# Two MLPs behind a retention layer: token blocks of 512 and 384, and the first weight conversions in another place

## The chip, the cores and the metric

One core of one Trainium2 chip. The time is the device time of one launch in microseconds (us). Three runs of the kernel before took 967.38, 970.62 and 971.07 us; the median is 970.62 us.

## The reference

```
scores = q @ k.T / sqrt(D);  ret = scores * Dmat        # Dmat = gamma_h ** (i - j) for i >= j, else 0
x  = heads side by side of ret @ v                      # 4 batches x 576 rows = 2304 tokens of 512
h  = x @ w_in;  x = (h * sigmoid(1.702 * h)) @ w_out                 # 512 -> 2048 -> 512
xn = x / sqrt(mean(x * x) + 1e-6) * rms_g
out = (silu(xn @ w_gate) * (xn @ w_val)) @ w_out2                    # 512 -> 1536 -> 512
```

All tensors are float32, and the weights too.

## The kernel before

Each matmul is done three times on fp32r operands: every operand is split into a high part and a rest, and `three` (lines 190 to 195) adds high x high, high x rest and rest x high into one PSUM tile. So one projection of 512 inputs onto 128 outputs is twelve matmuls whose moving operand is as wide as the token block.

**Blocks.** The first MLP goes through the 2304 tokens in blocks of 512, 448, 448, 448 and 448 (`BLOCKS`), the second in six blocks of 384 (`NB`). For each of the 16 (second MLP: 12) groups f of 128 hidden units, `m1_up` makes twelve matmuls into `h`, ACT and DVE apply the gate (`g`) and split it (`gh`, `gl`), and `m1_down` makes twelve more into four accumulators `acc`. `m2_up` makes twelve into `h` and twelve into `v`, and `m2_down` nine of 512 columns (three tiles of 128 tokens, three matmuls each). Down runs two groups behind up (`LAG`). Before each up, `w_rot` splits the group's output weights on ACT (`wrh`, line 186) and DVE (`wrl`, line 187).

**Attention.** The retention is done in units of at most 128 rows that end where a batch or a token block ends: 20 units, four of them of 64 rows. A unit is three phases: `a_trans` (transposes on TensorE, copies `kT` and `qT` on ACT), `a_scores` (matmuls of kT and qT, mask on DVE into `r`) and `a_out` (matmuls, then `x`, the carried state `S` and the split into `xh` and `xl`). Block 0's four units are done first; those of block n+1 are laid between the groups of block n by the table `gap` (lines 654 to 657): for block 0 phase i of the list goes to group 2 + i*14 // len(list).

**Weights.** They arrive as 64-bit words and are converted by `conv`: two passes on ACT (lines 159, 160), one on DVE (line 169), and for `in`, `gate` and `val` a cast and a difference on DVE (lines 176, 177). They are staged in six slots `sslots` and kept in 56 slots of 2 KB per partition. While block 0 runs, `conv_next(2)` converts one `in` and one `out` piece ahead of each group; the first two pieces are converted between attention phases (lines 640 and 642).

**Order.** Everything is written out by hand (`manual_schedule`): each engine works its queue off in the order of the code, and waits at the head of the queue hold all that is behind.

Of the kernel before, what the change touches and what calls it, by code (L numbers as in the profile page):

```python
# [8 lines left out]

F32 = mybir.dt.float32  # L10
F32R = mybir.dt.float32r
BF16 = mybir.dt.bfloat16
I32 = mybir.dt.int32
U32 = mybir.dt.uint32
U8 = mybir.dt.uint8
# [1 line left out]
ALU = mybir.AluOpType  # L17
PSUM = bass.MemoryType.PSUM

BLOCKS = (512, 448, 448, 448, 448)  # L20
NB = 384
XB = max(BLOCKS)
LAG = 2
NSLOT = 56
NMORE = 4
NSTG = 6
MAGIC = 0x5F3759DF
# [25 lines left out]
def kernel(  # L53
# [23 lines left out]
    KD = DM // 128  # L77
    NF1 = DF1 // 128
    NF2 = DF2 // 128
    NBLK = NT // NB  # L80
    N1 = len(BLOCKS)
    assert sum(BLOCKS) == NT
    TPB = NB // 128
# [3 lines left out]
    xp = ctx.enter_context(tc.tile_pool(name="xp", bufs=1))  # L87
    gp = ctx.enter_context(tc.tile_pool(name="gp", bufs=2))
    dram = ctx.enter_context(tc.tile_pool(name="dram", bufs=1, space=bass.MemoryType.DRAM))
    ps_acc = ctx.enter_context(tc.tile_pool(name="ps_acc", bufs=4, space=PSUM))  # L90
# [34 lines left out]
    staged = {}  # L125

    def w_free(key, f):
        wfree.extend(i for i, _ in W.pop((key, f)))

    def w_load(key, f):  # L130

# [18 lines left out]
    def words(key, f):  # L150
# [2 lines left out]
        b = sslots[:, i, :].bitcast(U8).rearrange("p (c t) -> p c t", t=8)  # L153
        return t[:, :, 0].bitcast(U32), t[:, :, 1], b[:, :, 3]

    def conv(pieces):
        for p in pieces:
            lo, hi, byte = words(*p)
            nc.scalar.activation(out=hi, in_=hi, func=AF.Prelu, scale=2.0 ** -112, alpha=-(2.0 ** 32))
            nc.scalar.activation(out=lo, in_=byte, func=AF.Copy, scale=1 / 32, bias=-31 / 64)  # L160
        for key, f in pieces:
            lo, hi, _ = words(key, f)
            if key in by_rows:
                W[key, f] = [w_slot("w")]
                w = W[key, f][0][1]
            else:
                W[key, f] = [w_slot("w") for _ in range(2)]
                w = gp.tile([128, 512], F32, tag="ww", name="ww", bufs=1)
            nc.vector.scalar_tensor_tensor(  # L169
                out=w.bitcast(U32), in0=hi.bitcast(U32), scalar=3, in1=lo,  # L170
                op0=ALU.logical_shift_left, op1=ALU.bitwise_or,
            )
            sfree.append(staged.pop((key, f)))
            if key not in by_rows:
                (_, wh), (_, wl) = W[key, f]
                nc.vector.tensor_copy(out=wh.bitcast(F32R), in_=w)  # L176
                nc.vector.tensor_tensor(out=wl.bitcast(F32R), in0=w, in1=wh, op=ALU.subtract)
# [26 lines left out]
    def block_tile(n):  # L204
        if n not in xt:
            xt[n] = (
                xp.tile([128, KD, BLOCKS[n % 2]], F32R, tag=f"xh{n % 2}", name="xh"),
                xp.tile([128, KD, BLOCKS[n % 2]], F32R, tag=f"xl{n % 2}", name="xl"),
            )
        return xt[n]  # L210

    aslots = {}
    hfree = deque()
    keep = [0]

    def a_tile(u, name):

        if len(wfree) > keep[0]:
            aslots[u, name], t = w_slot(name)
            return t  # L220
        if not hfree:
            i = sfree.popleft()
            hfree.extend([(i, 0), (i, 1)])
        i, j = aslots[u, name] = hfree.popleft()
        return sslots[:, i, j * 512:(j + 1) * 512]

    def a_free(u, *names):
        for nm in names:
            slot = aslots.pop((u, nm))
            if isinstance(slot, tuple):  # L230
                hfree.append(slot)
                if sum(i == slot[0] for i, _ in hfree) == 2:
                    hfree.remove((slot[0], 0))
                    hfree.remove((slot[0], 1))
                    sfree.append(slot[0])
            else:
                wfree.append(slot)

    def a_load(u, what="kqv"):
        b, s, c = units[u]  # L240
# [174 lines left out]
            )  # L415


    def halves(ids, c=NB):

        return [sslots[:, i, :2 * c].rearrange("p (k c) -> p k c", k=2) for i in ids]  # L420

# [17 lines left out]
    xraw = {}  # L439
    ssq = {}  # L440

    def norm_tile(name):
        return sp.tile([128, NB], F32, tag="norm", name=name, bufs=3)

    def m2_load(n):
        xraw[n] = [sfree.popleft() for _ in range(2)]
        for i, t in enumerate(halves(xraw[n])):
            nc.sync.dma_start(out=t, in_=y_d[:, 2 * i:2 * i + 2, n * NB:(n + 1) * NB])

    def m2_squares(n, i):  # L450

        y = halves(xraw[n])[i]
        if i == 0:
            ssq[n] = norm_tile("ssq"), norm_tile("sq")
        a, b = ssq[n]
        for j in range(2):
            o = a if i == j == 0 else b
            nc.gpsimd.tensor_tensor(out=o, in0=y[:, j, :], in1=y[:, j, :], op=ALU.mult)
            if o is b:
                nc.gpsimd.tensor_tensor(out=a, in0=a, in1=b, op=ALU.add)  # L460

    def m2_norm(n):

        y = halves(xraw[n])
        ps = ps_h.tile([128, XB], F32, tag="h", name="h")[:, :NB]
        nc.tensor.matmul(ps, ones, ssq.pop(n)[0], start=True, stop=True)
        m, r, t = (norm_tile(nm) for nm in ("m", "r", "t"))
        nc.vector.tensor_scalar(out=m, in0=ps, scalar1=1e-6, scalar2=None, op0=ALU.add)

        def guess():  # L470
# [21 lines left out]
    def m2_back(n):  # L492

        ids = xraw.pop(n)
        for i, t in enumerate(halves(ids)):
            nc.sync.dma_start(out=y_d[:, 2 * i:2 * i + 2, n * NB:(n + 1) * NB], in_=t)
        sfree.extend(ids)

    def m2_split(n, i):
        if n not in x2:  # L500
            x2[n] = (
                xp.tile([128, KD, BLOCKS[(N1 + n) % 2]], F32R, tag=f"xh{(N1 + n) % 2}", name="xh"),
                xp.tile([128, KD, BLOCKS[(N1 + n) % 2]], F32R, tag=f"xl{(N1 + n) % 2}", name="xl"),
            )
        xh, xl = x2[n]
        t = halves(xraw[n])[i]
        sfree.append(xraw[n][i])
        ks = slice(2 * i, 2 * i + 2)
        nc.scalar.copy(out=xh[:, ks, :NB], in_=t)
        nc.vector.tensor_tensor(  # L510
            out=xl[:, ks, :NB], in0=t, in1=xh[:, ks, :NB].bitcast(F32), op=ALU.subtract
        )

    def m2_up(n, f, fill):
        pg = ps_h.tile([128, XB], F32, tag="h", name="h")[:, :NB]
        proj(pg, "gate", f, x2[n], NB)
        g = hidden(F32, "g", NB, 2)
        nc.scalar.activation(out=g, in_=pg, func=AF.Sigmoid)  # L518
        nc.vector.tensor_tensor(out=g, in0=pg, in1=g, op=ALU.mult)  # L519
        pv = ps_v.tile([128, NB], F32, tag="v", name="v")  # L520
        proj(pv, "val", f, x2[n], NB)
        nc.vector.tensor_tensor(out=g, in0=pv, in1=g, op=ALU.mult)  # L522
        split_hidden((2, n, f), g, NB, fill)

    def m2_down(n, f):
        if f == 0:
            acc[n] = [ps_acc.tile([128, 512], F32, tag="acc", name="acc") for _ in range(4)]
        w = R.pop(("out2", f))
# [30 lines left out]
    with tc.manual_schedule():  # L559
# [220 lines left out]
```

## Time and profile before

| | |
|---|---|
| profiled execution, device time | 968.6 us |
| its span | 966.8 us |
| median of the three runs | 970.62 us |
| TensorE matmul busy | 953.6 us, 99% |
| DVE, ACT, POOL busy | 543.1, 376.7, 98.5 us |

The span goes from the first to the last instruction. TensorE's busy time is a union of overlapping matmuls, so the rate at which matmuls are issued has to be read from stretches that hold a known number of them.

### The profile page before, as it was taken

How to read it: one execution, taken by the hardware profiler on the slowest of the kernel's cores; microseconds unless marked ns; L12 is line 12 of the kernel's file. 1: busy time of each engine (PE TensorE's matmuls, PEld its weight loads, DVE VectorE, ACT ScalarE, POOL GpSimd, SP SyncE). 2: the span in 40 equal slices, each digit the busy share in tenths (PEclk: the TensorE clock that was granted, in tenths of full speed). 3: DMA queues.
4: the chain of work that ended last, by engine and by line, in shares of the span. 5: the costliest groups of instructions: out<-in, count | busy, mean ns of one | idle time of the engine just before them, and what ended most of it. 6: DMA issues, size and time to landing. Idle time of an engine off the chain costs nothing.

```text
span 966.8 us, 14045 instructions
## 1 busy us (share of the span) xinstructions
PE 953.6 (99%) x5654; PEld 860.8 (89%) x5654; DVE 543.1 (56%) x890; ACT 376.7 (39%) x688; POOL 98.5 (10%) x105
## 2 busy tenths in 40 slices
PE   9899999999999999999999999999999999999998
PEld 8687888889888989899999889999999999999997
DVE  3777754444446444367787785754654564554433
ACT  3566653334333433346665433232223223223322
POOL 3101111010311000100000330300110020000000
PEclk9999999999999999999999999999999999999999
DMA  9876502120211223006465301002001000000000
GB/s 233 211 218 180 148 17 77 33 52 18 85 34 50 65 55 126 23 36 199 122 194 190 89 1 66 1 1 66 1 1 55 12 1 11 23 1 1 33 1 33
DMA packets 92240, 66.77 MB, mean 69 GB/s; under 512 B 58896, under 2 KB 85648, under 8 KB 92176
## 3 DMA queue, kind: packets, MB, share of 16 engines
q1 hardware_dynamic: 92176, 65.89, 24.5%
q8 instruction: 44, 0.72, 0.3%
q14 instruction: 20, 0.16, 0.1%
HBM read 55.65 MB, written 10.22 MB: 68 GB/s over the span
## 4 chain that ended last, share of the span: by engine, by line
PE 89%; DVE 7%; ACT 2%; issue 1%; DMA 1%; DVEq 0%; ACTq 0%
PE h L193 12%; PE acc L195 11%; PE acc L194 11%; PE h L195 11%; PE h L194 11%; PE acc L193 11%; PE v L194 5%; PE v L195 5%; PE v L193 5%; PE at L286 2%; PE at L327 2%; PE at L261 2%; PE at L317 1%; DVE ww L169 1%; DVE w L176 1%
## 5 line engine op out<-in xcount | busy, mean ns | idle before, releaser
L193 PE MATMUL h<-xh,w 128*128 128x384 f32 (+2 forms) x608 | 223.0, 367 | 1.5 <-ACT xh L363 1.5
L194 PE MATMUL h<-xl,w 128*128 128x384 f32 (+2 forms) x608 | 216.2, 356 | 2.0 <-DVE xl L510 1.7
L195 PE MATMUL h<-xh,w 128*128 128x384 f32 (+2 forms) x608 | 216.7, 356 | 0.0
L378 ACT CAST gh<-g 128x384 fp32r<-128x384 f32 (+2 forms) x152 | 83.2, 547 | 252.6 <-DVE g L522 167.7
L380 DVE TENSOR_TENSOR gl<-g,gh 128x384 fp32r<-128x384 f32 (+2 forms) x152 | 94.2, 620 | 81.4 <-ACT gh L378 81.4
L187 DVE TENSOR_TENSOR wrl<-w,wrh 128x512 fp32r<-128x512 f32 x152 | 107.0, 704 | 56.2 <-ACT wrh L186 56.0
L193 PEld LDWEIGHTS h<-xh,w 128*128 128x128 f32 x608 | 114.6, 188 | 14.2 <-ACT xh L363 1.6
L194 PEld LDWEIGHTS h<-xl,w 128*128 128x128 f32 x608 | 114.7, 189 | 12.6 <-DVE xl L510 2.4
L195 PEld LDWEIGHTS h<-xh,w 128*128 128x128 f32 x608 | 114.4, 188 | 7.3
L186 ACT CAST wrh<-w 128x512 fp32r<-128x512 f32 x152 | 94.0, 619 | 68.2 <-PE acc L195 48.2
L195 PE MATMUL acc<-gh,wrl 128*128 128x448 f32 (+1 forms) x320 | 119.0, 372 | 0.6 <-DVE wrl L187 0.6
L194 PE MATMUL acc<-gl,wrh 128*128 128x448 f32 (+1 forms) x320 | 118.9, 371 | 0.0
L193 PE MATMUL acc<-gh,wrh 128*128 128x448 f32 (+1 forms) x320 | 118.8, 371 | 0.0
L402 DVE TENSOR_TENSOR g<-h,g 128x448 f32<-128x448 f32 (+1 forms) x80 | 50.8, 635 | 107.6 <-ACT g L401 107.5
L193 PE MATMUL v<-xh,w 128*128 128x384 f32 x288 | 96.2, 334 | 0.0
L195 PE MATMUL v<-xh,w 128*128 128x384 f32 x288 | 96.2, 334 | 0.0
L194 PE MATMUL v<-xl,w 128*128 128x384 f32 x288 | 96.2, 334 | 0.0
L401 ACT ACTIVATE g<-h 128x448 f32<-128x448 f32 (+1 forms) x80 | 44.3, 554 | 116.3 <-PE h L195 116.2
L194 PE MATMUL acc<-wrl,gh 128*128 128x512 f32 x216 | 85.4, 395 | 0.8 <-DVE wrl L187 0.8
L195 PE MATMUL acc<-wrh,gl 128*128 128x512 f32 x216 | 85.4, 396 | 0.0
L193 PE MATMUL acc<-wrh,gh 128*128 128x512 f32 x216 | 84.0, 389 | 0.0
L519 DVE TENSOR_TENSOR g<-h,g 128x384 f32<-128x384 f32 x72 | 40.0, 555 | 60.3 <-ACT g L518 60.3
(82 smaller groups left out, 1224.5 us busy)
## 6 DMA issues: line engine op xcount, KB each, us to landing
sslots<-in_moe_w_out_dram SPq DMA_DIRECT2D x28, 512.0 KB, 4.4
sslots<-in_moe_w_in_dram SPq DMA_DIRECT2D x16, 512.0 KB, 4.3
sslots<-in_moe_w_gate_dram SPq DMA_DIRECT2D x12, 512.0 KB, 4.5
sslots<-in_moe_w_val_dram SPq DMA_DIRECT2D x12, 512.0 KB, 5.4
sslots<-y_d SPq DMA_DIRECT2D x14, 384.0 KB, 3.9
out_dram<-sslots SPq DMA_DIRECT2D x18, 256.0 KB, 2.1
k<-in_k_dram SPq DMA_DIRECT2D x16, 256.0 KB, 3.8
q<-in_q_dram SPq DMA_DIRECT2D x16, 256.0 KB, 4.7
```

The costliest lines, as they stand in the source:

```text
L186: nc.scalar.copy(out=wh.bitcast(F32R), in_=w)
L187: nc.vector.tensor_tensor(out=wl.bitcast(F32R), in0=w, in1=wh, op=ALU.subtract)
L193: nc.tensor.matmul(ps, lh, rh, start=first, stop=False)
L194: nc.tensor.matmul(ps, lh, rl, start=False, stop=False)
L195: nc.tensor.matmul(ps, ll, rh, start=False, stop=last)
L261: nc.tensor.transpose(pt[i][:, p * c:(p + 1) * c], t[:c, 2 * p:2 * p + 2, :].rearrange("p h d -> p (h d)"), ident[:c, :c],)
L286: nc.tensor.matmul(sc[j][:c, p * c:(p + 1) * c], kT[r0:r0 + 64, p, :c], qT[r0:r0 + 64, p, :c], start=True, stop=True,)
L378: nc.scalar.copy(out=gh, in_=g)
L380: nc.vector.tensor_tensor(out=gl, in0=g, in1=gh.bitcast(F32), op=ALU.subtract)
L401: nc.scalar.activation(out=g, in_=ps, func=AF.Sigmoid, scale=1.702)
L402: nc.vector.tensor_tensor(out=g, in0=ps, in1=g, op=ALU.mult)
L519: nc.vector.tensor_tensor(out=g, in0=pg, in1=g, op=ALU.mult)
```

## The change

Both MLPs use five blocks of 512 and 384 tokens. The first two conversions each move one place back: that of `in` 0 from behind `a_out(2)` to behind `a_scores(3)`, that of `in` 1 to behind `a_out(3)`. The warm-up loses its fp32r and bf16 matmuls and has ten fp32 ones instead of eight. Since both x buffers are now 512 wide, one weight slot goes (55 instead of 56), and the last two `out2` pieces are kept in halves of a staging slot. Shapes follow the block in the second MLP (`norm_tile`, `rows_of`, `halves`, four tiles per block in `m2_down` and `m2_end` where a block has 512 tokens). The blocks end at tokens 512, 1024, 1408 and 1792, so block 1 has five attention units instead of four, block 2 three.

```diff
-BLOCKS = (512, 448, 448, 448, 448)
-NB = 384
-XB = max(BLOCKS)
+BLOCKS = (512, 512, 384, 384, 512)
+BLOCKS2 = (512, 512, 512, 384, 384)
+XB = 512
-NSLOT = 56
+NSLOT = 55
...
+    def in_half(key, f):
+
+        return key == "out2" and f >= NF2 - 2
...
-                W[key, f] = [w_slot("w")]
+                W[key, f] = [half_slot() if in_half(key, f) else w_slot("w")]
...
-        pv = ps_v.tile([128, NB], F32, tag="v", name="v")
-        proj(pv, "val", f, x2[n], NB)
+        pv = ps_v.tile([128, XB], F32, tag="v", name="v")[:, :c]
+        proj(pv, "val", f, x2[n], c)
...
-        for t in range(TPB):
+        for t in range(BLOCKS2[n] // 128):
...
-        for _ in range(8):
+        for _ in range(10):
             nc.tensor.matmul(heat[:, :128], ones, ones[:, :128], start=True, stop=True)
-        (i0, warm_r), (i1, warm_b) = w_slot("warm_r"), w_slot("warm_b")
...
-        for c in (512, 384, 256, 128):
-            for _ in range(3):
-                nc.tensor.matmul(heat[:, :c], warm_r[:, :128], warm_r[:, :c], start=True, stop=True)
-        for c in (512, 128):
-            for _ in range(3):
-                nc.tensor.matmul(heat[:, :c], warm_b[:, :128], warm_b[:, 512:512 + c], start=True, stop=True)
-        wfree.extend((i0, i1))
...
         a_out(2, ACC)
-        conv_next(1, N2)
         a_scores(3, ACC)
         conv_next(1, N2)
         a_out(3, ACC)
+        conv_next(1, N2)
```

On DVE, at the end of the attention that goes ahead of block 0, the kernel before has these rows (`r` is the masked score of unit 3, `ww` and `w` are the conversion of a weight piece, `x` and `S` belong to `a_out(3)`):

```order
L360 TENSOR_TENSOR S<-S,sdec 128x256
L169 SCALAR_TENSOR_TENSOR ww<-sslots 128x512
L176 CAST w<-ww 128x512
L177 TENSOR_TENSOR w<-ww,w 128x512
L297 TENSOR_TENSOR r_387<-at,mask 128x512
L297 TENSOR_TENSOR r_388<-at,mask 128x512
L169 SCALAR_TENSOR_TENSOR ww<-sslots 128x512
L176 CAST w<-ww 128x512
L177 TENSOR_TENSOR w<-ww,w 128x512
L348 TENSOR_TENSOR x<-at,qdec 128x512
```

The changed kernel has these in the same place:

```order
L365 TENSOR_TENSOR S<-S,sdec 128x256
L302 TENSOR_TENSOR r_358<-at,mask 128x512
L302 TENSOR_TENSOR r_359<-at,mask 128x512
L190 SCALAR_TENSOR_TENSOR ww<-sslots 128x512
L197 CAST w<-ww 128x512
L198 TENSOR_TENSOR w<-ww,w 128x512
L353 TENSOR_TENSOR x<-at,qdec 128x512
L364 TENSOR_TENSOR S<-at,S 128x256
L365 TENSOR_TENSOR S<-S,sdec 128x256
L369 TENSOR_TENSOR xl<-x,xh 128x4x128
L190 SCALAR_TENSOR_TENSOR ww<-sslots 128x512
```

Both conversions have moved behind what they stood ahead of: the first behind `r`, the second behind `x`, `S` and `xl`.

On TensorE, in block 0, the kernel before has the scores of unit 4 (a unit of 64 rows, `L286` with 64x64) behind a whole down, with the 24 matmuls of up 2 and down 0 between them and the unit's transposes:

```order
L193 MATMUL acc<-gh,wrh 128x512
L194 MATMUL acc<-gl,wrh 128x512
L195 MATMUL acc<-gh,wrl 128x512
L286 MATMUL at<-qT,kT 64x64 x8
L193 MATMUL h<-xh,w 128x512
```

In the changed kernel the list of block 1 has 15 phases instead of 12, and `gap` puts the first two of them at group 2:

```order
L215 MATMUL h<-xl,w 128x512
L216 MATMUL h<-xh,w 128x512
L266 MATMUL at<-ident,k 128x64 x4
L266 MATMUL at<-ident,q 128x64 x4
L291 MATMUL at<-qT,kT 64x64 x8
L214 MATMUL h<-xh,w 128x512
```

The scores now follow the transposes with nothing between. What they read, kT and qT, is copied on ACT, where the queue of the changed kernel reads from up 0 on (the kernel before has the same operations in the same order there):

```order
L406 ACTIVATE g<-h 128x512
L383 CAST gh<-g 128x512
L180 ACTIVATE sslots<-sslots 128x512
L181 ACTIVATE sslots<-sslots 128x512
L180 ACTIVATE sslots<-sslots 128x512
L181 ACTIVATE sslots<-sslots 128x512
L207 CAST wrh<-w 128x512
L406 ACTIVATE g<-h 128x512
L383 CAST gh<-g 128x512
L273 COPY kT<-at 128x4x64
L274 COPY qT<-at 128x4x64
```

The copies stand behind the whole of group 1; it is the TensorE rows that have moved against them.

## Rows read from the trace of the kernel before

**Rows 1.** The page's part 1: busy us (share of the span) x instructions of each engine.

```profile
PE 953.6 (99%) x5654; PEld 860.8 (89%) x5654; DVE 543.1 (56%) x890; ACT 376.7 (39%) x688; POOL 98.5 (10%) x105
```

**Rows 2.** Waits of PE in the whole span: us in total, times, longest.

```profile
PE at L327 <- DVE r L297: 2.5, 1, 2.5
PE h L194 <- DVE xl L510: 1.7, 2, 1.3
```

**Rows 3.** Windows on PE: stretch, its us, busy us (x instructions), granted clock, DMA.

```profile
408.73:498.01 89.28, 89.28 (x433) 1.00 0.42 132
293.91:296.35 2.44, 2.44 (x13) 1.00 0.90 203
130.63:133.35 2.72, 2.72 (x13) 1.00 0.00 0
614.40:616.49 2.09, 2.09 (x14) 1.00 0.00 0
612.30:674.97 62.67, 62.67 (x332) 1.00 0.08 26
605.41:681.23 75.82, 75.82 (x399) 1.00 0.07 22
```

**Rows 4.** Timeline 0 to 48: start us, us, engine, line, operation [idle before <-releaser].

```profile
7.17 0.99 PE L612 MATMUL heat<-warm_b 128*128 128x512 bf16 x6
...
23.81 0.42 DVE L360 TENSOR_TENSOR S<-S,sdec 128x256 f32<-128x256 f32 x1
...
25.27 0.76 DVE L169 SCALAR_TENSOR_TENSOR ww<-sslots 128x512 uint32<-128x512 uint32 x1 [1.03 <-ACT sslots L160]
...
27.13 1.28 DVE L297 TENSOR_TENSOR r<-at,mask 128x512 f32<-128x512 f32 x2
...
28.33 0.68 DVE L169 SCALAR_TENSOR_TENSOR ww<-sslots 128x512 uint32<-128x512 uint32 x1
...
30.12 0.68 DVE L348 TENSOR_TENSOR x<-at,qdec 128x512 f32<-128x512 f32 x1
...
31.51 0.50 PE L193 MATMUL h<-xh,w 128*128 128x512 f32 x1 [1.49 <-ACT xh L363]
```

**Rows 5.** Window on PE after the first matmuls of block 0.

```profile
33.36:36.77 3.41, 3.41 (x10) 0.50 0.67 217
```

**Rows 6.** The timeline 24 to 48 further on: groups 0 to 2 of block 0.

```profile
33.29 1.04 POOL L270 TENSOR_TENSOR v<-v,vdec 64x512 f32<-64x512 f32 x1 [7.81 <-DMA v<-in_v_dram]
...
33.34 1.27 DVE L176 CAST w<-ww 128x512 fp32r<-128x512 f32 x1
...
37.90 0.62 ACT L378 CAST gh<-g 128x512 fp32r<-128x512 f32 x1 [0.76 <-DVE g L402]
...
38.42 0.68 ACT L159 ACTIVATE sslots<-sslots 128x512 f32<-128x512 f32 x1
...
39.69 0.69 DVE L169 SCALAR_TENSOR_TENSOR ww<-sslots 128x512 uint32<-128x512 uint32 x1 [0.44 <-ACT sslots L160]
...
42.69 0.68 DVE L402 TENSOR_TENSOR g<-h,g 128x512 f32<-128x512 f32 x1
...
43.41 0.62 ACT L378 CAST gh<-g 128x512 fp32r<-128x512 f32 x1 [1.64 <-DVE g L402]
...
44.20 0.38 ACT L269 COPY qT<-at 128x256 f32<-128x256 f32 x1
...
45.66 0.68 PE L286 MATMUL at<-qT,kT 64*64 64x64 f32 x16
...
46.28 0.50 PE L193 MATMUL h<-xh,w 128*128 128x512 f32 x1
```

**Rows 7.** Timelines on PE at 82, at 550 and at 579: matmuls that waited.

```profile
82.97 0.50 PE L195 MATMUL acc<-gh,wrl 128*128 128x512 f32 x1 [0.62 <-DVE wrl L187]
...
550.47 0.50 PE L194 MATMUL acc<-wrl,gh 128*128 128x512 f32 x1 [0.80 <-DVE wrl L187]
...
579.76 0.45 PE L194 MATMUL h<-xl,w 128*128 128x384 f32 x1 [1.32 <-DVE xl L510]
```

More of the change, by code (lines that the diff above doesn't have):

```diff
@@ L11 @@
 F32R = mybir.dt.float32r
-BF16 = mybir.dt.bfloat16
 I32 = mybir.dt.int32
@@ L79 @@
     NF2 = DF2 // 128
-    NBLK = NT // NB
+    NBLK = len(BLOCKS2)
     N1 = len(BLOCKS)
-    assert sum(BLOCKS) == NT
-    TPB = NB // 128
+    assert sum(BLOCKS) == sum(BLOCKS2) == NT
     const = ctx.enter_context(tc.tile_pool(name="const", bufs=1))
     sp = ctx.enter_context(tc.tile_pool(name="sp", bufs=1))
-    xp = ctx.enter_context(tc.tile_pool(name="xp", bufs=1))
+    xp = ctx.enter_context(tc.tile_pool(name="xp", bufs=2))
     gp = ctx.enter_context(tc.tile_pool(name="gp", bufs=2))
@@ L111, with half_slot, give @@
     sfree = deque(range(NSTG))
+    hfree = deque()
+    def half_slot():
+        if not hfree:
+            i = sfree.popleft()
+            hfree.extend([(i, 0), (i, 1)])
+        i, j = hfree.popleft()
+        return (i, j), sslots[:, i, j * 512:(j + 1) * 512]
+    def give(slot):
+        if not isinstance(slot, tuple):
+            wfree.append(slot)
+            return
+        hfree.append(slot)
+        if sum(i == slot[0] for i, _ in hfree) == 2:
+            hfree.remove((slot[0], 0))
+            hfree.remove((slot[0], 1))
+            sfree.append(slot[0])
     ap = tc.tile_pool(name="ap", bufs=1)
@@ L127, in w_free @@
     def w_free(key, f):
-        wfree.extend(i for i, _ in W.pop((key, f)))
+        for i, _ in W.pop((key, f)):
+            give(i)
     def w_load(key, f):
@@ L206, in block_tile @@
             xt[n] = (
-                xp.tile([128, KD, BLOCKS[n % 2]], F32R, tag=f"xh{n % 2}", name="xh"),
-                xp.tile([128, KD, BLOCKS[n % 2]], F32R, tag=f"xl{n % 2}", name="xl"),
+                xp.tile([128, KD, XB], F32R, tag="xh", name="xh"),
+                xp.tile([128, KD, XB], F32R, tag="xl", name="xl"),
             )
@@ L212 @@
     aslots = {}
-    hfree = deque()
-    keep = [0]
     def a_tile(u, name):
[L218 to L225, printed above, removed]
+        aslots[u, name], t = w_slot(name) if wfree else half_slot()
+        return t
     def a_free(u, *names):
         for nm in names:
[L229 to L237, printed above, removed]
+            give(aslots.pop((u, nm)))
     def a_load(u, what="kqv"):
@@ L415, in m1_down, with halves @@
             )
-    def halves(ids, c=NB):
+    def halves(ids, c):
         return [sslots[:, i, :2 * c].rearrange("p (k c) -> p k c", k=2) for i in ids]
@@ L440, with norm_tile, rows_of @@
     ssq = {}
-    def norm_tile(name):
-        return sp.tile([128, NB], F32, tag="norm", name=name, bufs=3)
+    def norm_tile(name, c):
+        return sp.tile([128, XB], F32, tag="norm", name=name, bufs=3)[:, :c]
+    def rows_of(n):
+        t0 = sum(BLOCKS2[:n])
+        return slice(t0, t0 + BLOCKS2[n])
     def m2_load(n):
         xraw[n] = [sfree.popleft() for _ in range(2)]
-        for i, t in enumerate(halves(xraw[n])):
-            nc.sync.dma_start(out=t, in_=y_d[:, 2 * i:2 * i + 2, n * NB:(n + 1) * NB])
+        for i, t in enumerate(halves(xraw[n], BLOCKS2[n])):
+            nc.sync.dma_start(out=t, in_=y_d[:, 2 * i:2 * i + 2, rows_of(n)])
     def m2_squares(n, i):
-        y = halves(xraw[n])[i]
+        y = halves(xraw[n], BLOCKS2[n])[i]
         if i == 0:
-            ssq[n] = norm_tile("ssq"), norm_tile("sq")
+            ssq[n] = norm_tile("ssq", BLOCKS2[n]), norm_tile("sq", BLOCKS2[n])
         a, b = ssq[n]
@@ L462, in m2_norm @@
     def m2_norm(n):
-        y = halves(xraw[n])
-        ps = ps_h.tile([128, XB], F32, tag="h", name="h")[:, :NB]
+        c = BLOCKS2[n]
+        y = halves(xraw[n], c)
+        ps = ps_h.tile([128, XB], F32, tag="h", name="h")[:, :c]
         nc.tensor.matmul(ps, ones, ssq.pop(n)[0], start=True, stop=True)
-        m, r, t = (norm_tile(nm) for nm in ("m", "r", "t"))
+        m, r, t = (norm_tile(nm, c) for nm in ("m", "r", "t"))
         nc.vector.tensor_scalar(out=m, in0=ps, scalar1=1e-6, scalar2=None, op0=ALU.add)
@@ L494, in m2_back @@
         ids = xraw.pop(n)
-        for i, t in enumerate(halves(ids)):
-            nc.sync.dma_start(out=y_d[:, 2 * i:2 * i + 2, n * NB:(n + 1) * NB], in_=t)
+        for i, t in enumerate(halves(ids, BLOCKS2[n])):
+            nc.sync.dma_start(out=y_d[:, 2 * i:2 * i + 2, rows_of(n)], in_=t)
         sfree.extend(ids)
@@ L501, in m2_split @@
             x2[n] = (
-                xp.tile([128, KD, BLOCKS[(N1 + n) % 2]], F32R, tag=f"xh{(N1 + n) % 2}", name="xh"),
-                xp.tile([128, KD, BLOCKS[(N1 + n) % 2]], F32R, tag=f"xl{(N1 + n) % 2}", name="xl"),
+                xp.tile([128, KD, XB], F32R, tag="xh", name="xh"),
+                xp.tile([128, KD, XB], F32R, tag="xl", name="xl"),
             )
         xh, xl = x2[n]
-        t = halves(xraw[n])[i]
+        c = BLOCKS2[n]
+        t = halves(xraw[n], c)[i]
         sfree.append(xraw[n][i])
         ks = slice(2 * i, 2 * i + 2)
-        nc.scalar.copy(out=xh[:, ks, :NB], in_=t)
+        nc.scalar.copy(out=xh[:, ks, :c], in_=t)
         nc.vector.tensor_tensor(
-            out=xl[:, ks, :NB], in0=t, in1=xh[:, ks, :NB].bitcast(F32), op=ALU.subtract
+            out=xl[:, ks, :c], in0=t, in1=xh[:, ks, :c].bitcast(F32), op=ALU.subtract
         )
     def m2_up(n, f, fill):
-        pg = ps_h.tile([128, XB], F32, tag="h", name="h")[:, :NB]
-        proj(pg, "gate", f, x2[n], NB)
-        g = hidden(F32, "g", NB, 2)
+        c = BLOCKS2[n]
+        pg = ps_h.tile([128, XB], F32, tag="h", name="h")[:, :c]
+        proj(pg, "gate", f, x2[n], c)
+        g = hidden(F32, "g", c, 2)
         nc.scalar.activation(out=g, in_=pg, func=AF.Sigmoid)
         nc.vector.tensor_tensor(out=g, in0=pg, in1=g, op=ALU.mult)
-        pv = ps_v.tile([128, NB], F32, tag="v", name="v")
-        proj(pv, "val", f, x2[n], NB)
+        pv = ps_v.tile([128, XB], F32, tag="v", name="v")[:, :c]
+        proj(pv, "val", f, x2[n], c)
         nc.vector.tensor_tensor(out=g, in0=pv, in1=g, op=ALU.mult)
-        split_hidden((2, n, f), g, NB, fill)
+        split_hidden((2, n, f), g, c, fill)
     def m2_down(n, f):
@@ L535, in m2_end @@
         a = acc.pop(n)
-        for t in range(TPB):
+        for t in range(BLOCKS2[n] // 128):
             i = sfree.popleft()
@@ L542, in m2_end @@
                 nc.vector.tensor_copy(out=o, in_=a[t])
-            r0 = n * NB + t * 128
+            r0 = rows_of(n).start + t * 128
             nc.sync.dma_start(out=out[r0:r0 + 128, :], in_=o)
@@ L585, in conv_next @@
             while len(entered) < k and len(to_conv) > upto and to_conv[0] in staged:
-                need += 1 if to_conv[0][0] in by_rows else 2
-                if need > len(wfree):
+                need += 0 if in_half(*to_conv[0]) else 1 if to_conv[0][0] in by_rows else 2
+                if need > len(wfree) or in_half(*to_conv[0]) and not (hfree or sfree):
                     break
```

4 lines of the change are left out of this document (removed).

## The prediction

> **What bounds the kernel now.** I read the page first: TensorE is busy 99% of the span, DVE 56% and ACT 39% [rows 1]. The reader is to see that no other engine can be the bound over a stretch of any length, only at places. Then the waits of TensorE [rows 2]: the two longest kinds make 4.2 us, one at the end of the first attention units, one at a block boundary of the second MLP. So the time is the number of matmuls by the interval at which they are issued, plus a few places. The windows give the interval, because each holds a known number of matmuls [rows 3]: 432 matmuls of 448 columns take 89.28 us, 0.2067 us each, and a quieter dozen of 448 takes 2.44 us, 0.2033 each; twelve of 512 take 2.72 us, 0.2267; twelve of 384 take 2.09 us, 0.174. Ten groups of the second MLP take 62.67 us, 6.267 each, and a whole block 75.82 us, which is 0.6 us more than twelve groups. Last I read the timeline of the first 48 us [rows 4 to 6], since the change moves work there.
>
> **The widths in the first MLP.** A block has 16 groups of 24 matmuls, 384. Before: 384 x 0.2267 + 1536 x 0.205, the middle between the two rows of 448, is 87.1 + 314.9 = 402.0 us. After: three blocks of 512 and two of 384, 1152 x 0.2267 + 768 x 0.174 = 261.2 + 133.6 = 394.8 us. So -7.1 us. The columns are the same in number; what goes is that 448 columns cost more than half way between 384 and 512 (0.200). Bounds: with 0.2033 throughout -4.6, with 0.2067 throughout -9.7.
>
> **The widths in the second MLP.** Before, 72 groups x 6.267 = 451.2 us. A group has 24 up matmuls of 384 columns, 4.18 us, so its nine down matmuls take 2.09, 0.232 each. A group of 512 tokens has 24 x 0.2267 + 12 x 0.232 = 8.23 us. After: 36 x 8.23 + 24 x 6.267 = 446.7, so -4.5 us. Here 288 up matmuls fewer carry the gain. Bounds: 0 if the up matmuls of 512 run at 0.232 as those of down do, -5 if nothing is lost beside them. One block boundary fewer: -0.6 us.
>
> [...]
>
> **The places in the second MLP.** At 550 us down waits 0.8 us for `wrl` [rows 7], because in the first block DVE also converts weights. In blocks of 512 DVE's work for a group grows only in its gate part, TensorE's by 8.23/6.267 = 1.31; I take the wait as gone, -0.8 (bounds -0.8 and +1). At 579 us the second block waits for its normalised input [rows 7]. That chain is DVE work on tiles that are wider by 4/3, hidden behind TensorE work that is longer by 1.31; I cost it at nothing (bounds -1.7, its whole price in rows 2, and +1.5). The staging slot that goes to `out2` leaves `m2_end` three slots for four tiles; the fourth copy then waits for an output DMA, behind it on DVE stand the gate operations of the next group, and the next down into that accumulator comes a whole up, 5.4 us, later. At nothing.
>
> **The start.** The warm-up of before ends at 8.2 us [rows 4]. The shorter one frees TensorE earlier by up to 3 us, and bounds of that edit are -3 and 0. I take 0: the loads cover it, as POOL's idle time until `v` lands shows [rows 6], and a transpose that comes before its data waits. Without that cover all of the start would move up with it. The order of DVE is what counts. Before, `r` of unit 3 starts at 27.13, behind the conversion that began at 25.27 [rows 4]. Now it follows `S`, which ends at 24.23, and ends 1.28 us later, 25.5. The conversion behind it takes what the one between 28.33 and 30.12 took, 1.79 us, so `x` starts at 27.3 instead of 30.12. From `x` to the first matmul of block 0 it is 1.39 us [rows 4]: 28.7 instead of 31.51. That is 2.8 us earlier for TensorE. It does not last, because of the new order of the attention phases.
>
> TensorE does up 0, up 1 and the transposes of unit 4 and stands at that unit's scores at about 35.5. These read `qT`, and ACT copies it behind the whole of group 1. That moment is worked out along ACT and DVE. `xh` leaves ACT's head about 28.5; the two passes of `in` 1 take 1.27 us until DVE can begin (38.42 to 39.69 [rows 6]), 29.8. Then DVE converts `in` 1 and `in` 2, 1.79 each, and `out` 0, 0.6, and reaches `g` of group 0 at 34.0. From `g` to `gh` it is 0.72 (42.69 to 43.41), 34.7; from one `gh` to the next 5.51 (37.90 to 43.41), 40.2; from `gh` to the end of `qT` 1.17, 41.4 [rows 6]. One step can be longer: at 33.34 a cast of DVE took 1.27 us with POOL's work on `v` beside it [rows 6], about 0.8 more than the share it has in the 1.79. So the scores start between 41.4 and 42.2; I take 41.8. TensorE waits there some 6 us.
>
> [...]
>
> Compare where the same work is done. Before, scores of unit 4, up 0 to 2 and down 0 are behind TensorE at 46.28 [rows 6]. Now: 41.8 + 0.62 for the scores (45.66 to 46.28) + 2.83 for up 2 (twelve intervals and 0.11 for the change of kind) + 2.72 for down 0 = 48.0, 1.7 us later. From there TensorE is the late one: `wrl` of group 0 is there at about 40, five us before its down. So the wait at 82.97 for `wrl` [rows 7], 0.6 us by its row and 0.8 between the starts, goes: +0.9 us net, with bounds 0.4 and 1.3.
>
> Then the clock. [...] Bounds 0 and 3.4 us (twice); I take +1.5.
>
> **Sum.** -7.1 - 4.5 - 0.6 - 0.8 + 0.9 + 1.5 = -10.6 us against the profiled execution's 968.6 us: 958.0. The median of the runs shown, 970.62, lies 2.0 us above it; taken to the median, 960.0 us.
>
> **The rivals.**
> *The width doesn't matter.* The cost is per column, and 448 is dear because of what runs beside it. Then the two MLP terms are 0, and -0.6 - 0.8 + 2.4 = +1.0 gives 971.6. For it: the dozen of 448 at 0.2033 [rows 3] shows that the interval does move with the surroundings. [...]
> *The start keeps its gain.* No wait at the scores, no fall of the clock: -13.0 for the rest, then -2.8, -0.8 and -1.6, together -18.2, 952.4. Against it stands ACT's queue, which has `qT` behind `gh` of group 1.
> *ACT and DVE bound block 0.* A group takes them 5.51 us, TensorE 5.44 and the attention. If POOL costs DVE 0.84 us in each of 14 groups, 11.8 us, less the lead of 5.3, that is +6.5: 966.5. For it: attention units are five instead of four in this block. Against: of the first groups only a few show such a step.
> *Slower: the clock stays down after the wait at the scores.* One matmul of 512 then costs 0.2 us more. From about 80 matmuls at the lower level on the kernel is slower than before by over 0.5%; at 100 it would be 960.0 + 18.5 = 978.5. Against: before, it came back after ten matmuls, and nothing pauses TensorE behind that place.
>
> **How the numbers follow.** Forecast 0.74, its own range 956 to 965; width doesn't matter 0.09; start keeps its gain 0.06; ACT and DVE bound 0.08; clock stays down 0.03. The range 954 to 967 takes in the forecast with its bounds, and half of the third and fourth case each. Half a per cent, 4.9 us, is about what a measurement of this kernel can tell from no change: faster means below 965.8. Forecast and kept start give nearly all of faster, with part of the fourth case: 0.83. No change: the first rival and the rest of the fourth, 0.14. Slower 0.03.
>
> **What would show it.** Windows in blocks 2 and 3 with 24 matmuls of 384 in 4.2 us, and groups of 8.2 us in the second MLP: widths right. A wait of TensorE for `qT` (the copy on ACT) of about 6 us before 42, with a granted clock of 0.5 near it: the start right. `r` of unit 3 before 24.5 and the first matmul of block 0 near 28.7: the moved conversions right. No wait for `wrl` at 82. The forecast is wrong if matmuls of 512 in the second MLP take 0.232, if waits for `wrl` or `gl` come up in block 0, or if a wait for a weight piece appears where staging has a slot less.

## The result: 958.24 us, 1.2% faster

Four runs of the changed kernel took 957.86 to 958.44 us, median 958.24; the kernel before, on the same chip, 967.38 to 971.07, median 970.58. The ratio is 0.9879 (95% interval 0.9858 to 0.9901). The forecast was 960.0 us, its range 954 to 967. The profiled executions, 968.6 and 958.32 us, differ by 10.3 us; the forecast's sum was -10.6. The four runs of the kernel before spread over 3.7 us, and 2 of the 12.3 us between the medians are that spread. The total fits better than its terms: the start came out 1.3 us dearer than forecast, the second MLP 1.8 cheaper.

In the experiments below, one execution of a changed kernel (1559 us; with it that kernel's median would be 958.91) and two of the kernel before (1565 and 1168 us) ran at a mean granted clock of 0.56 to 0.75 and are left out of the medians.

### The profile page after: what moved, and what is told of

The parts are those of the page before. It is cut to its first block, busy times and chain, and to the rows that moved or that the text cites. A ratio compares the mean times of both kernels' runs of the same rounds, so it can differ in the third digit from the quotient of the medians.

```text
span 956.5 us, 13270 instructions
## 1 busy us (share of the span) xinstructions
PE 940.3 (98%) x5350; PEld 812.2 (85%) x5350; DVE 530.7 (55%) x826; ACT 366.4 (38%) x648; POOL 97.0 (10%) x96
## 4 chain that ended last, share of the span: by engine, by line
PE 94%; DVE 2%; SPq 1%; DMA 1%; issue 0%; ACT 0%; DVEq 0%; ACTq 0%
PE h L214 13%; PE acc L216 12%; PE acc L215 12%; PE h L215 12%; PE h L216 12%; PE acc L214 12%; PE v L214 5%; PE v L216 5%; PE v L215 5%; PE at L291 2%; PE at L332 2%; PE at L322 1%; PE at L266 1%; SPq L249 1%; DMA q<-in_q_dram 1%; PE at L343 1%
## 5 line engine op out<-in xcount | busy, mean ns | idle before, releaser
L214 PE MATMUL h<-xh,w 128*128 128x512 f32 (+1 forms) x560 | 214.1, 382 | 1.5 <-ACT xh L368 1.5
L215 PE MATMUL h<-xl,w 128*128 128x512 f32 (+1 forms) x560 | 207.7, 371 | 2.4 <-DVE xl L521 2.0
L216 PE MATMUL h<-xh,w 128*128 128x512 f32 (+1 forms) x560 | 207.8, 371 | 0.0
L383 ACT CAST gh<-g 128x512 fp32r<-128x512 f32 (+1 forms) x140 | 81.0, 578 | 236.0 <-DVE g L534 156.9
L385 DVE TENSOR_TENSOR gl<-g,gh 128x512 fp32r<-128x512 f32 (+1 forms) x140 | 93.3, 666 | 79.5 <-ACT gh L383 79.5
L216 PE MATMUL acc<-gh,wrl 128*128 128x512 f32 (+1 forms) x320 | 117.6, 368 | 0.0
L215 PE MATMUL acc<-gl,wrh 128*128 128x512 f32 (+1 forms) x320 | 117.5, 367 | 0.0
L214 PE MATMUL acc<-gh,wrh 128*128 128x512 f32 (+1 forms) x320 | 117.5, 367 | 0.0
L407 DVE TENSOR_TENSOR g<-h,g 128x512 f32<-128x512 f32 (+1 forms) x80 | 50.9, 636 | 98.6 <-ACT g L406 98.5
L214 PE MATMUL v<-xh,w 128*128 128x512 f32 (+1 forms) x240 | 88.1, 367 | 0.0
L215 PE MATMUL v<-xl,w 128*128 128x512 f32 (+1 forms) x240 | 88.1, 367 | 0.0
L216 PE MATMUL v<-xh,w 128*128 128x512 f32 (+1 forms) x240 | 88.1, 367 | 0.0
L531 DVE TENSOR_TENSOR g<-h,g 128x512 f32<-128x512 f32 (+1 forms) x60 | 38.2, 637 | 65.2 <-ACT g L530 65.1
```

What stands on the lines that cost most here:

```text
L214: nc.tensor.matmul(ps, lh, rh, start=first, stop=False)
L215: nc.tensor.matmul(ps, lh, rl, start=False, stop=False)
L216: nc.tensor.matmul(ps, ll, rh, start=False, stop=last)
L383: nc.scalar.copy(out=gh, in_=g)
L385: nc.vector.tensor_tensor(out=gl, in0=g, in1=gh.bitcast(F32), op=ALU.subtract)
L407: nc.vector.tensor_tensor(out=g, in0=ps, in1=g, op=ALU.mult)
```

## The profile after

First the page's span and part 1 (busy us, share of the span, instructions), then PE's waits in the whole span (us in total, times, longest).

```profile
span 956.5 us, 13270 instructions
PE 940.3 (98%) x5350; PEld 812.2 (85%) x5350; DVE 530.7 (55%) x826; ACT 366.4 (38%) x648; POOL 97.0 (10%) x96
```

```profile
PE at L291 <- ACT qT L274: 5.8, 2, 5.0
PE h L215 <- DVE xl L521: 2.0, 2, 1.5
PE h L214 <- ACT xh L368: 1.5, 1, 1.5
```

TensorE has 304 instructions fewer than in [rows 1]. The wait for `r` [rows 2] is gone, and one for `qT` has come; the wait for `xl` in the second MLP is still there, 2.0 instead of 1.7. No wait for `wrl` is left, neither of the two in [rows 7].

**Where the time went.** Windows between places with equal work behind TensorE: the first matmul of block 0; the end of scores of unit 4, up 0 to 2 and down 0; the first `v` matmul of the second MLP; the end. Columns: stretch, its us, busy us (x instructions), granted clock, DMA share, GB/s. The kernel before:

```profile
31.51:46.28 14.77, 14.44 (x73) 0.88 0.72 208
46.28:502.58 456.30, 455.68 (x2883) 1.00 0.33 91
502.58:963.10 460.52, 458.02 (x2399) 1.00 0.10 31
```

The changed kernel:

```profile
28.48:50.83 22.35, 16.97 (x73) 0.77 0.81 225
50.83:500.08 449.25, 449.25 (x2879) 1.00 0.32 91
500.08:952.87 452.79, 450.75 (x2109) 1.00 0.09 30
```

TensorE begins block 0 3.03 us earlier (28.48 against 31.51). The first stretch then takes 7.58 us more with the same 73 instructions, the rest of the first MLP 7.05 less, the second MLP 7.73 less: -10.23, which is the difference of the spans but for 0.1. The first `v` is not quite the seam between the MLPs: the first twelve matmuls of the second lie ahead of it (0.6 us more than before, as they are 512 wide now), the last 24 down matmuls of the first behind it (0.5 us more). The two nearly cancel.

**The start.** The timeline of the changed kernel (start us, us, engine, line, operation, [idle before <- releaser]):

```profile
24.09 1.29 DVE L302 TENSOR_TENSOR r<-at,mask 128x512 f32<-128x512 f32 x2
...
28.48 0.50 PE L214 MATMUL h<-xh,w 128*128 128x512 f32 x1 [1.50 <-ACT xh L368]
...
36.68 0.41 PE L266 MATMUL at<-ident,q 64*128 64x64 f32 x4
...
40.91 0.62 ACT L383 CAST gh<-g 128x512 fp32r<-128x512 f32 x1 [1.65 <-DVE g L407]
...
41.70 0.38 ACT L274 COPY qT<-at 128x256 f32<-128x256 f32 x1
...
42.13 1.12 PE L291 MATMUL at<-qT,kT 64*64 64x64 f32 x16 [5.05 <-ACT qT L274]
```

`r` follows at 24.09 (before: 27.13 [rows 4]) and the first matmul 3 us earlier. TensorE has transposed unit 4 by 37.1 and then waits 5.05 us: ACT copies `qT` behind `gh` of group 1. Windows on PE around it:

```profile
30.46:33.87 3.41, 3.41 (x10) 0.52 0.69 231
40.70:47.53 6.83, 5.40 (x27) 0.51 0.75 195
```

The granted clock fell twice, to 0.52 and 0.51 in these windows: in up 0, as before [rows 5], and in the wait for `qT`, from where it lasted into up 2. Up 2 took 4.8 us with it (43.18 to 47.98).

**The widths.** Windows of the changed kernel: 24 matmuls of 384 columns (first MLP), twelve of down in a block of 512 tokens, a whole group of such a block, nine of down in a block of 384:

```profile
403.11:407.27 4.16, 4.16 (x26) 1.00 0.00 0
662.26:664.98 2.72, 2.72 (x13) 1.00 0.00 0
662.26:670.42 8.16, 8.16 (x37) 1.00 0.00 0
865.07:867.15 2.08, 2.08 (x11) 1.00 0.00 0
```

A matmul of 384 takes 0.1733 us (4.16/24) and one of 512 0.2267 (2.72/12), in down of the second MLP too; there the forecast had taken 0.232 from nine matmuls in 2.09 us [rows 3]. In blocks of 384 nine still take 2.08, 0.231 each. A whole group takes 8.16 us and not 8.23.

## The experiments

Each is the changed kernel with one edit, beside the kernel before on the same chip. The changed kernel's 958.24 is the point of comparison; its four runs lie within 0.6 us. It was not run again on those chips, where the kernel before had medians of 969.60, 968.88 and 968.63 instead of 970.58, so a difference between medians of 1 us or so says little by itself. Stages of the traces are the safer measure: the rest of the first MLP takes 449.25 us in the changed kernel and in all five other traces that leave it as it is.

### The second MLP in six blocks again

```diff
-BLOCKS2 = (512, 512, 512, 384, 384)
+BLOCKS2 = (384, 384, 384, 384, 384, 384)
```

> The changed kernel with the second MLP back in six blocks of 384 tokens, all else as changed. Width theory: the second MLP's matmuls give back what they gained, 4.8 us of up and 1.8 us of down, and one block boundary more 0.6; the wait for xl at the first boundary may stay at 2: about 965.0 us (963.5 to 966.5). Rival, cost per column: only the boundary comes back, about 959. In the trace the nine down matmuls of a group of 384 should take 231 ns each again, and those of a 512 block 227.

Measured: 964.19 us (963.89 to 964.34). Windows on PE in its trace: nine down matmuls, a whole group (24 of up, nine of down), and the second MLP from the first `v` to the end:

```profile
662.36:664.44 2.08, 2.08 (x11) 1.00 0.00 0
664.44:670.70 6.26, 6.26 (x34) 1.00 0.75 251
498.76:958.84 460.08, 458.39 (x2399) 1.00 0.09 30
```

Nine take 2.08 again. The stage takes 460.08 us, 7.3 more than the 452.79 of the changed kernel; 0.8 of that comes back ahead of it, for the most part because the first twelve up matmuls are 384 wide, and 0.5 in the start. Cost per column, which allows 0.6, is out.

### 448 and 448 instead of 384 and 512

```diff
-BLOCKS = (512, 512, 384, 384, 512)
+BLOCKS = (512, 512, 384, 448, 448)
```

> The changed kernel with the first MLP's last two blocks of 448 and 448 tokens instead of 384 and 512; the same number of instructions of each kind in TensorE, columns equal in sum. Width theory: 768 matmuls at 0.205 to 0.207 instead of 384 at 0.2267 and 384 at 0.174, +3.6 to +4.9 us: 961.8 to 963.1. Rival, cost per column: 0, 958.2 within 0.7.

Measured: 961.25 us (961.05 to 962.33), +3.0. Windows on PE: 48 matmuls of 448, and the first MLP from the place after down 0 to the end:

```profile
441.07:451.00 9.93, 9.93 (x50) 1.00 0.68 217
49.90:503.36 453.46, 453.46 (x2879) 1.00 0.32 90
```

One of 448 takes 0.2067 us (four dozens in 9.92). The stage is 4.21 us longer than 449.25 with the same 2879 instructions. 0.5 of it is no matter of price: the 24 down matmuls that fall behind the stage's end are 448 wide here and 512 there, so the stage has more columns, and what follows is 0.5 shorter. That leaves +3.7, at the lower edge of the width theory's +3.6 to +4.9. The execution as a whole was only 2.7 longer, because its start was 0.9 us shorter: the scores of unit 4 began at 42.07 as in the changed kernel, but the stretch in which the granted clock was 0.51 ran from 38.87 to 45.70 instead of from 40.70 to 47.53.

### The first MLP in its old blocks

```diff
-BLOCKS = (512, 512, 384, 384, 512)
+BLOCKS = (512, 448, 448, 448, 448)
```

> The changed kernel with the first MLP back in blocks of 512 and four of 448; then block 1 has four attention units, so that no group has transposes and scores of one unit together. Width theory: +6.9 us for the first MLP. Theory of the start: the wait of 5.05 us for qT and the second stretch at the lower clock (1.8 us) go, of which the chain over ACT and DVE gives back some 2 to 3: -4 to -5 us. Together 960 to 961.5. Rival (the wait isn't due to the doubled phase but to the chain alone): wait and stretch stay, 965. Rival (cost per column): 954.

Measured: 958.78 us (958.67 to 959.04), 0.5 above the changed kernel and below the 960 expected. So the new widths of the first MLP, worth some 7 us by themselves, bring nearly nothing in this kernel. The trace of a second run shows why.

> The first MLP in blocks of 512 and four of 448 once more, for its trace (the median of the earlier run was 958.91). Theory: in the trace TensorE has no wait of 5 us for qT and no low clock behind it, the first matmul of the second MLP starts within 1 us of the changed kernel's 500.1, and blocks 1 to 4 of the first MLP take 6 to 7 us longer; the start is 5 to 6 us shorter. Rival: the wait is there, and 448 costs 0.200 as its columns say.

Measured: 958.72 us (958.63 to 958.89). The timeline on PE:

```profile
36.80 0.41 PE L266 MATMUL at<-ident,q 64*128 64x64 f32 x4
...
42.97 0.68 PE L291 MATMUL at<-qT,kT 64*64 64x64 f32 x16
43.58 0.50 PE L214 MATMUL h<-xh,w 128*128 128x512 f32 x1
...
80.64 0.50 PE L216 MATMUL acc<-gh,wrl 128*128 128x512 f32 x1 [0.89 <-DVE wrl L208]
```

Block 1 has four units here, the scores stand one group behind the transposes, and up 2 and down 0 lie between: no wait, no low clock behind it. The work that the changed kernel has done at 50.83 is done at 43.58, 7.25 us earlier. Even against 46.28 of the kernel before [rows 6] that is 2.7 earlier; my rival "the start keeps its gain" is what happens where block 1 has four units. From 43.58 to the first `v` at 501.15 it then takes 457.57 us instead of 449.25, 8.3 more; 0.9 of that is the wait for `wrl` at 80.64, which is back now that TensorE is early. The fifth unit, which the new boundaries bring, cost what the widths earned.

### The conversions back in their old place

```diff
+        conv_next(1, N2)
         a_scores(3, ACC)
         conv_next(1, N2)
         a_out(3, ACC)
-        conv_next(1, N2)
```

> The changed kernel with only the first two weight conversions back in their old places (behind the output of units 2 and, for the second, the scores of unit 3). Theory of the start: r of unit 3 falls back to about 27.1 us, the first matmul of block 0 to about 31.5, and the chain over the gate of groups 0 and 1 to the copy qT moves with it, so that the scores of unit 4 start about 44.5 instead of 42.1: +2 to +3 us, 960.2 to 961.2. Rival: the wait for qT is set by the conversions alone, whose work is the same, and swallows the place where the first two stand: within 0.5 of 958.2.

Measured: 959.78 us (958.65 to 960.85), +1.5, between the two. The timeline of its trace:

```profile
26.86 1.28 DVE L302 TENSOR_TENSOR r<-at,mask 128x512 f32<-128x512 f32 x2
...
31.23 0.49 PE L214 MATMUL h<-xh,w 128*128 128x512 f32 x1 [1.49 <-ACT xh L368]
...
42.98 1.12 PE L291 MATMUL at<-qT,kT 64*64 64x64 f32 x16 [4.78 <-ACT qT L274]
```

The first matmul comes 2.75 us later, the scores only 0.85: both theories had a part. The executions spread over 2.2 us, and the one of the trace is the fastest: there the work up to down 0 is done at 51.14, 0.31 later, which is the rival's figure. So the +1.5 of the medians does not settle between them. Most of what the moved conversions gain at 28 us is swallowed by the wait at 42.

### One attention phase per group

```diff
-gap.setdefault((2 if n == 0 else 1) + i * (NF1 - 2) // max(1, len(todo)), []).append(t)
+gap.setdefault(1 + i * (NF1 - 1 if n == 0 else NF1 - 2) // max(1, len(todo)), []).append(t)
```

> The changed kernel with the 15 attention phases of block 1 laid one per group on groups 1 to 15 of block 0 (as changed: two on group 2, then one each). Theory of the start: the wait of 5.05 us comes from transposes and scores of one unit standing in the same group, with the copy qT behind gh of group 1 on ACT; a group apart, qT follows gh of group 0 and is there at about 37 us, before TensorE's scores; wait and the stretch at the lower clock behind it go: -5 to -7, 951 to 953.5 us. Rival, the chain of ACT and DVE bounds block 0 (5.5 us from one gh to the next): the wait comes back at up or down of groups 2 to 5, as waits for g, gl or wrl, and the gain is under 2: 956.3 to 958.5.

Measured: 951.44 us (951.34 to 951.67), -6.8. Its timeline:

```profile
32.07 0.41 PE L266 MATMUL at<-ident,q 64*128 64x64 f32 x4
...
35.33 0.62 ACT L383 CAST gh<-g 128x512 fp32r<-128x512 f32 x1 [2.85 <-DVE g L407]
...
36.12 0.38 ACT L274 COPY qT<-at 128x256 f32<-128x256 f32 x1
...
36.55 0.68 PE L291 MATMUL at<-qT,kT 64*64 64x64 f32 x16 [1.11 <-ACT qT L274]
```

The window on PE from there to the place after down 0:

```profile
36.55:43.28 6.73, 6.61 (x41) 1.00 0.82 200
```

`qT` follows `gh` of group 0, up 1 covers most of the time until then, and 1.11 us of wait are left; the clock stays at 1.00 behind it. No other wait of TensorE comes up in block 0, so the chain of ACT and DVE does not bound it.

### Work in the wait

```diff
+                if fn is a_trans and u == 4:
+                    idle = ps_acc.tile([128, 512], F32, tag="acc", name="idle")
+                    for _ in range(20):
+                        nc.tensor.matmul(idle, xt[0][0][:, 0, :128], xt[0][0][:, 0, :], start=True, stop=True)
```

> The changed kernel with twenty extra fp32r matmuls of 512 columns behind the transposes of unit 4, into an accumulator tile that nothing reads: TensorE works during most of its wait for qT. Clock theory: the fall to the lower level behind the wait is due to the pause; with work in it the clock stays, the scores take 0.7 instead of 1.1 us and nine intervals 0.227 instead of 0.427: -2.2 us, 956.0 (at least -1). Rival: the fall comes whatever TensorE does there, or the wait's end comes later by the extra work: 958.2 or up to 1 more.

Measured: 955.78 us (955.75 to 957.42), -2.5. Two rows of its timeline and the window from the first extra matmul to the end of up 2:

```profile
36.73 4.84 PE L652 MATMUL idle<-xh 128*128 128x512 f32 x20
...
41.94 0.68 PE L291 MATMUL at<-qT,kT 64*64 64x64 f32 x16 [0.37 <-ACT qT L274]
```

```profile
36.73:45.41 8.68, 8.31 (x51) 1.00 0.86 235
```

The scores start 0.2 us earlier and take 0.68 instead of 1.12 us, and the clock stays at 1.00. From their start to the place after down 0 it is 6.28 us instead of 8.70: 2.4 us is the price of the clock alone, and 4.84 us of useless matmuls bring it back.

### The normalisation one group earlier

```diff
-                    if f == f0 + (4 if n == 0 else 3):
+                    if f == f0 + 3:
                         spread += m2_norm(n + 1)
-                    if f == NF2 - 1:
+                    if f == NF2 - (2 if n == 0 else 1):
                         m2_split(n + 1, 0)
```

> The changed kernel with the normalisation of the second MLP's block 1 one group earlier (its sums behind the third group after the load instead of the fourth, the split before group 10 instead of 11). In the trace of the changed kernel POOL squares block 2 from 587.7 to 599 us, and beside it DVE's scaling takes 1.5 us a piece instead of 1.06 on average and its xl 2.15 instead of 1.18. Theory: the first boundary's wait of 2.3 us (xl behind that) is only a matter of its place in the queue; a group earlier it is hidden: -2.0 to -2.4, 955.9 to 956.2. Rival: DVE and POOL are still in each other's way, and gl or wrl of groups 9 to 11 come late instead: within 0.7 of 958.2.

Measured: 955.05 us (954.58 to 955.49), -3.2. No wait of TensorE behind 50 us is left in its trace. Of the 3.0 us between the spans 2.6 lie in the second MLP and 0.4 in the start. DVE's work takes as long as in the changed kernel, only 8.6 us earlier:

```profile
579.68 6.01 DVE L495 SCALAR_TENSOR_TENSOR sslots<-sslots,rg,r 128x512 f32<-128x512 f32 x4
```

### POOL behind DVE

```diff
             ssq[n] = norm_tile("ssq", BLOCKS2[n]), norm_tile("sq", BLOCKS2[n])
+            if n > 1:
+                z = x2[n - 1][1][:, 3, :1].bitcast(F32)
+                nc.gpsimd.tensor_tensor(out=warm, in0=z, in1=z, op=ALU.mult)
```

> The changed kernel with one tiny POOL operation more ahead of the squares of blocks 2 to 4 of the second MLP; it reads the last column of xl of the block before, so that POOL squares the next block only behind DVE's split. The order on DVE is as changed. Theory of contention: without POOL beside it DVE's scaling takes about 0.7 us a piece instead of 1.5 and xl about 1.2 instead of 2.15, the chain to xl ends some 5 us earlier, and the wait of 2.3 us at the first boundary goes: 955.5 to 956.2, like the run that moved the normalisation (955.05). Rival: the durations are DVE's own, and the wait at the boundary stays: within 0.7 of 958.2.

Measured: 955.94 us (955.29 to 956.02), -2.3. The changed kernel's timeline ahead of the boundary at 596 us:

```profile
587.65 1.49 POOL L467 TENSOR_TENSOR ssq<-sslots 128x512 f32<-128x512 f32 x1 [35.50 <-DVE t L490]
...
588.28 6.01 DVE L495 SCALAR_TENSOR_TENSOR sslots<-sslots,rg,r 128x512 f32<-128x512 f32 x4
594.21 1.78 DVE L385 TENSOR_TENSOR gl<-g,gh 128x512 fp32r<-128x512 f32 x1
595.92 4.29 DVE L521 TENSOR_TENSOR xl<-sslots,xh 128x1024 fp32r<-128x1024 f32 x2
...
596.97 2.15 POOL L469 TENSOR_TENSOR ssq<-ssq,sq 128x512 f32<-128x512 f32 x1
...
598.03 0.50 PE L215 MATMUL h<-xl,w 128*128 128x512 f32 x1 [1.46 <-DVE xl L521]
```

The same with POOL held back (lines behind 463 are three higher):

```profile
588.47 2.74 DVE L498 SCALAR_TENSOR_TENSOR sslots<-sslots,rg,r 128x512 f32<-128x512 f32 x4
591.13 0.69 DVE L385 TENSOR_TENSOR gl<-g,gh 128x512 fp32r<-128x512 f32 x1
591.73 2.35 DVE L524 TENSOR_TENSOR xl<-sslots,xh 128x1024 fp32r<-128x1024 f32 x2
...
594.16 0.58 POOL L466 TENSOR_TENSOR warm<-xl 128x1 f32<-128x1 f32 x1 [41.75 <-DVE xl L524]
...
594.70 1.03 POOL L470 TENSOR_TENSOR ssq<-sslots 128x512 f32<-128x512 f32 x1
```

The same DVE work takes 2.74, 0.69 and 2.35 us instead of 6.01, 1.78 and 4.29, and the wait is gone; the second MLP is 2.6 us shorter, as much as in the run before. So the wait has two sides, and either edit removes it: POOL squares the next block beside this chain and makes 12.1 us out of 5.8, and the chain's place in the queue leaves too little TensorE work to hide that. Beside each other both took longer: a scaling takes 1.50 us instead of 0.69, and POOL's first square beside it 1.49 instead of the 1.03 that it takes when held back. What makes them slower cannot be told from these rows.

### The old warm-up

```diff
-        for _ in range(10):
+        for _ in range(8):
...
+        for c in (512, 384, 256, 128):
+            for _ in range(3):
+                nc.tensor.matmul(heat[:, :c], warm_r[:, :128], warm_r[:, :c], start=True, stop=True)
...
```

> The changed kernel with the old warm-up (eight fp32 matmuls, twelve in fp32r and six in bf16). Theory: the loads cover it; TensorE leaves it at 8 us instead of 5.5, waits less for q and k, and the scores of unit 3 start 0.1 us later: within 0.5 of 958.2. Rival: the shorter warm-up gave back part of its 2.5 us: 959.5 to 960.7. Second rival: the longer one keeps the clock up in the first units: 957 or less.

Measured: 958.08 us (957.29 to 958.71). No difference beyond the spread. In its trace the first matmul of block 0 starts at 28.93, 0.45 us later than in the changed kernel. TensorE comes to the first transposes 2.8 us later (8.29 instead of 5.50) and has no wait for the loads of q and k, which took 1.7 us in the changed kernel: the loads cover most of it.

### Both gains together

The edits of "One attention phase per group" and of "The normalisation one group earlier".

> Both edits that gained by themselves: one attention phase per group in block 0, and the normalisation of block 1 one group earlier. They touch stretches that are 450 us apart, so their gains add: 951.4 - 3.2 = 948.2 (947.5 to 949). Rival: part of the 3.2 us was difference between executions at the start, where the clock's low stretches fall; then 951.4 - 2.4 = 949.0 or a little more.

Measured: 948.90 us (948.78 to 949.08), ratio to the kernel before 0.9795 (0.9782 to 0.9809). It beats both kernels, by 19.7 us (968.63 on its chip) and by 9.3. The rival's 949.0 was the better figure: the boundary was worth 2.5 us, and 0.4 of the rest of the 3.2 was the start of that execution.

## Why the prediction was right, and where it was not

Per stage, the forecast against the windows:

| stage | forecast | measured |
|---|---|---|
| start, to the place after down 0 | 48.0 + 1.5 - 46.28 = +3.2 | +4.55 (50.83 - 46.28) |
| rest of the first MLP | -7.1 - 0.8 = -7.9 | -7.05 |
| second MLP | -4.5 - 0.6 - 0.8 = -5.9 | -7.73 |

**First MLP's widths, -7.1: right.** -7.05 holds 0.8 of the vanished wait for `wrl` and, by adding up the intervals, 0.4 more in attention; with the 0.6 and 0.5 at the seam about -6.8 is left for the widths. That 448 is dear and not only its surroundings was an assumption; the pair of 448 showed it with +3.7 us.

**Second MLP's widths, -4.5: right in kind, too small.** The sum has a slip: 24 x 0.2267 + 12 x 0.232 is 8.225 us and not 8.23, 0.2 over 36 groups. The term that was mis-sized is the price of 0.232 for each down matmul. In groups of 512 it is 0.2267: 36 groups x 12 x 0.0053 = 2.3 us more gain. I had read 0.232 as the cost of 512 columns in that stage, although 512 had 0.2267 elsewhere [rows 3]. The run with six blocks of 384 shows that it belongs to the groups of 384. Why nine matmuls of 512 columns are slower behind 24 of 384 stays open. With the slip, these 2.3 us and 0.4 more at the first boundary, the forecast's -5.9 becomes -8.0; the windows give -7.6 with the seam taken out, so 0.4 us stay unaccounted.

**The wait at the first boundary at nothing: nearly right as a difference, cause missed.** I expected DVE's wider tiles to be hidden behind TensorE's longer groups, so the sum counts no change. That was nearly so: from start to start the twelve matmuls there took 4.32 us instead of 2.08 before, and 5.34 instead of 2.72 now, 0.4 more. What I had not looked for is POOL beside DVE, and the kernel before has it too:

```profile
571.86 1.14 POOL L458 TENSOR_TENSOR ssq<-sslots 128x384 f32<-128x384 f32 x1 [25.03 <-DVE t L480]
...
572.35 4.56 DVE L485 SCALAR_TENSOR_TENSOR sslots<-sslots,rg,r 128x384 f32<-128x384 f32 x4
```

That is 1.14 us a scaling, where the operations on 384 columns just ahead of it take 0.56. Holding POOL back in the changed kernel took 2.3 us off.

**The start, +0.9 and +1.5: mechanism right, 1.3 us too small.** `r` began at 24.09 and block 0 at 28.48, as worked out. `qT` ended at 42.08, within 41.4 to 42.2. The wait was 5.05 us and not 6, since the clock fell in up 0 as well (0.52) and the wait swallowed that; with the pair of 448, where it was 1.00 there, the wait was 6.64. The clock was low already in the scores (1.05 us between starts instead of the 0.62 counted) and then in up 2 (4.80 instead of 2.83): 2.4 us, within the bound of 3.4. No run shows the 1.5 taken for it, which was my estimate; the stretch before [rows 5] gives 1.6, its 3.41 us being eight intervals that are 0.2 us longer than 0.2267. The wait ended 0.3 late (42.13 instead of 41.8).

**Nothing for the warm-up and for the staging slot: right.** In the changed trace DVE's copy in `m2_end` does wait for output DMAs, 4.2 us in three waits, and no wait of TensorE follows.

**To the median.** The 2.0 us that I added were a property of three runs: the changed kernel's profiled run lies 0.1 from its median. That, and +1.3, +0.85 and -1.8 in the stages, make the total look better than its parts.

## What to carry to other kernels

When block sizes change, count what else hangs on them: here a fifth attention unit put two dependent phases into one slot of a table, and its wait with the clock behind it cost 7 us, as much as the better widths earned. Before a wait is put down to its place in a queue alone, compare the durations of the instructions in front of it with the same ones elsewhere; an engine that has nothing to do may be running ahead beside them (here POOL: DVE's scaling took 1.50 us instead of 0.69). A matmul's price is taken from a stretch of the same kind and neighbours, not from the same number of columns alone (here 0.2267 us for 512, and 0.231 behind 24 of 384).

## What the runs showed of the hardware

- Matmuls on fp32r operands, each with its weight load, took 0.1733, 0.2067 and 0.2267 us for 384, 448 and 512 columns: 448 lies 0.0067 above the middle, and 0.0033 in the dozen at 0.2033 [rows 3]. 512 took 0.231 in groups with 24 of 384.
- In six traces TensorE waited 4.78 to 6.79 us for `qT`, and the scores behind the wait took 1.12 us, the first matmuls of up 2 0.43 us apart. The granted clock was 0.51 from 40.70 to 47.53 in the changed kernel (wait until 42.13) and from 38.87 to 45.70 with the pair of 448 (wait until 42.07). With matmuls in the wait (0.37 us left), or with one attention phase per group (a wait of 1.11 us), the scores took 0.68 us and the clock behind them was 1.00. From the start of the scores to the place after down 0 it was 8.70 us in the changed kernel and 7.83 with the pair of 448, against 6.28 with matmuls in the wait: the low clock cost 2.4 and 1.6 us there.
- Behind the 1.5-us wait for `xh` the matmuls of up 0 were 0.43 us apart instead of 0.23 for a stretch in five of eight traces of kernels alike in that place; in the changed kernel the granted clock was 0.52 there, with the pair of 448, one without it, 1.00 (30.46 to 33.87 in both). Where a long wait for `qT` followed, it swallowed this: the scores began at 42.07 with the pair of 448 and at 42.13 in the changed kernel.
- DVE's scaling and `gl` on 512 columns took 0.69 us alone and 1.5 to 1.8 beside POOL operations on as many.
